# A fused attention and two-MLP kernel: the first six attention tiles put in source order, with small steps moved from GpSimd to VectorE

## The chip, the cores and the metric

The kernel runs as one program on one core of a Trainium2 chip. The metric is the time of one execution in device microseconds; a kernel's time is the median of its runs.

## What is computed

Inputs are float32, the MLP weights float64. Three stages follow one another on 4 sequences of 768 tokens with 8 heads of 48 (a model width of 384).

```python
# 1. linear attention with a decaying state, per batch and head
for t in range(768):
    cur = outer(u * k[t], v[t])
    y[t] = r[t] @ (state + cur)
    state = w[:, None] * state + outer(k[t], v[t])
# 2. a gated MLP with a 3-tap convolution over time
h = maximum(x @ w_in, 0)                       # 384 -> 1024
conv = sum(conv_w[j] * shifted(h, j - 1) for j in range(3))
x = (h * sigmoid(conv)) @ w_out                # 1024 -> 384
# 3. layer norm, MLP, residual
xn = (x - mean) / sqrt(var + 1e-6) * g_ln
out = x + maximum(xn @ w_ch1, 0) @ w_ch2       # 384 -> 1536 -> 384
```

## The kernel before

Attention is done in 24 tiles of 128 tokens, 6 for each batch. The first MLP (`mixer1`) works on 8 blocks of 384 tokens, which are three attention tiles each, and the second (`mixer2`) on 6 blocks of 512. Products that need full precision are split into a high and a low part, and three matmuls are made of each.

*Attention tiles.* A generator, `attention`, yields after each half tile; the main loop calls `step()` to take one. The first six tiles (`n < LIGHT`, LIGHT is 6) go through `light_tile`. For such a tile VectorE (DVE in the profile) scales r and k by a decay table (`rk`, line 347), multiplies them (`z`, line 302) and makes the decayed k (`kks`, line 247, `decayed_k`). TensorE (PE) makes the dot products `dps` and the diagonal `pa8`. ScalarE (ACT) copies them (`aT`, `a8`), GpSimd (POOL) masks `aT` and makes `va`. PE adds them up in `yps`; ACT writes the high part `xh`, PE takes it away with the matrix `minus`, and ACT writes the low part `xl`. `halos` then copies single columns between neighbouring blocks, since the convolution needs one token on each side: when tile 3 is done, its first column goes into the last column of block 0's `xh` and `xl`. `state_update` makes the next state: `pst` on PE, `sn` on DVE, the decayed state `sw` (line 396, on POOL for the first six tiles), and two ACT copies `sbds`.

*Weights.* The float64 weights are decoded on the chip in 22 pieces (`wjob`). A piece is loaded into `st`; ACT takes the magnitude of its upper words (Abs, `wdec<-st`), an engine clamps it (`magnitude`, TENSOR_SCALAR `wdec<-wdec` in float32), DVE shifts it (TENSOR_SCALAR in int32) and combines it twice (SCALAR_TENSOR_TENSOR), ACT writes the high part (`wih`, `woh`), DVE the low part (`wil`, `wol`). The next piece's Abs and clamp are issued between the second combination and the high part. `me` is a piece's number: 0 to 2 are the first half of `w_in`, 3 is the first rows of `w_out`, 4 to 6 the second half of `w_in`, 7 to 9 the rest of `w_out`, 10 to 21 belong to the second MLP. In the kernel before, pieces 0 to 3 are clamped on DVE and the others on POOL. `wdo` takes decode steps; in the start loop two are taken after each `step()`, until piece 3 is done, and two at each call in block 0.

*Order.* Each engine works through its own queue in order. Instructions issued through the wrappers `vo`, `ao`, `so`, `go` and `pe` (of the class `InOrder`) are kept behind the instruction that was issued just before them on their engine. All of PE's instructions and the weight decode are issued so. Those issued through the plain names `v_`, `a_`, `g_` and `nc.sync` may be put earlier by a scheduler at compile time, as soon as its own estimate has their inputs ready, but no later than the next kept one. The attention's DVE, ACT and POOL instructions and the tile loads are of this kind. Loads are issued by SP.

*Start.* `tables` loads the small inputs and tiles 0 to 2, builds the decay tables, and makes `tku[:, 0]` through a PE transpose (`ptk`, from `tkw`) and two ACT copies (line 697); `decayed_k(0)` needs this table. Then comes:

```python
    cst = tables()
    decayed_k(0)
    while finished[0] < EARLY - 1:   # EARLY is 4
        step()
        wdo(2, wo_job[0])
```

Of the kernel before, what the change touches and what calls it, by code (L numbers as in the profile page):

```python
# [32 lines left out]
NP = H // 2  # L33
# [15 lines left out]
def body(ctx, tc, r, k, v, w, u, w_in, conv_w, w_out, g_ln, w_ch1, w_ch2, rkT, krv, small, out):  # L49
# [89 lines left out]
    def wjob(src, n, hi, lo, scale=None):  # L139

        st, mag = [], []

        def load():
            st.append(io.tile([128, 2 * WN], I32, tag="st", name="st", bufs=3))
            dst = st[0][:, 0:2 * n]
            if len(src.shape) == 3:
                dst = dst.rearrange("p (a n) -> p a n", a=src.shape[1])
            so.dma_start(out=dst, in_=src.bitcast(I32))

        def ahead():  # L150
            if not mag:
                mag.append(magnitude(st[0], n, vo if me < 4 else go))

        def steps():
            ahead()
            t = mag[0]
            yield from decode(st[0], n, t)
            if me + 1 < min(len(wjobs), w_loaded[0]):
                wjobs[me + 1][2]()
            if len(src.shape) == 3:  # L160
                t = t.rearrange("p (a n) -> p a n", a=src.shape[1])
            kw = {} if scale is None else {"scale": gl[:, scale:scale + 1]}
            ao.activation(out=hi, in_=t, func=AF.Copy, **kw)
            yield
            if scale is None:
                vo.tensor_tensor(out=lo, in0=t, in1=hi.bitcast(F32), op=ALU.subtract)
            else:
                vo.scalar_tensor_tensor(out=lo, in0=t, scalar=kw["scale"], in1=hi.bitcast(F32),
                                        op0=ALU.mult, op1=ALU.subtract)
        me = len(wjobs)  # L170
        wjobs.append((load, steps(), ahead))
        return len(wjobs) - 1

# [70 lines left out]
    def decayed_k(n):  # L244

        if n < LIGHT:
            v_.tensor_tensor(out=kks[:, n % 2, 0, :, 0:D], in0=loaded[n][1], in1=tku[:, 0], op=ALU.mult)
            return
        v_.tensor_tensor(out=kks[:, n % 2, :, :, 0:D], in0=loaded[n][1].unsqueeze(1).to_broadcast([128, 2, H, D]), in1=tku,  # L249
                         op=ALU.mult)  # L250
# [28 lines left out]

    def halos(n, xh, xl):  # L280
        i, j = n % TPB, n // TT
        for t, e in ((xh, 0), (xl, 1)):
            if i == 0:
                g_.memset(t[:, :, 0:1].bitcast(F32), 0.0)
            if i == TPB - 1:
                g_.memset(t[:, :, T + 1:T + 2].bitcast(F32), 0.0)
            if n % TT == 0 and i > 0:
                g_.tensor_copy(out=xT[j - 1][e][:, :, T + 1:T + 2], in_=t[:, :, 1:2].bitcast(F32))  # L288
                g_.tensor_copy(out=t[:, :, 0:1], in_=xT[j - 1][e][:, :, T:T + 1].bitcast(F32))

    def dot_products(rT, kT):
        dps = [ps_a.tile([128, NP, C], F32, tag="pa", name="dps") for _ in range(2)]
# [5 lines left out]

    def light_tile(n, rk, vt, py, py_tag):
        rT, kT = rk[:, 0], rk[:, 1]  # L300
        z = ap.tile([PR, NP, C], F32, tag="z", name="z", bufs=2)
        v_.tensor_tensor(out=z, in0=rT, in1=kT, op=ALU.mult)
        yield

        dps = dot_products(rT, kT)
        pb, pb_tag = (ps_m, "m") if n < EARLY else (ps_a, "pa")
        pa8 = pb.tile([128, 512], F32, tag=pb_tag, name="pa8")[:, 0:H]
        for p in range(NP):
            pe.matmul(pa8[:, 2 * p:2 * p + 2], lhsT=z[:, p, :], rhs=ub[:, 2 * p:2 * p + 2], start=True, stop=True)
        aT = ap.tile([128, 2, NP, C], F32, tag="aT", name="aT", bufs=2)  # L310
        a8 = sp.tile([128, H, 1], F32, tag="a8", name="a8", bufs=2)
        for q in range(2):
            a_.activation(out=aT[:, q], in_=dps[q], func=AF.Copy)
            g_.affine_select(out=aT[:, q], in_=aT[:, q], compare_op=ALU.is_gt, fill=0.0, base=0,
                             pattern=[[0, NP], [1, C]], channel_multiplier=-1)
        a_.activation(out=a8.rearrange("x h o -> x (h o)"), in_=pa8, func=AF.Copy)
        va = ap.tile([128, H, D], F32, tag="av", name="va", bufs=2)
        g_.tensor_tensor(out=va, in0=vt[:, :, 0:D], in1=a8.to_broadcast([128, H, D]), op=ALU.mult)
        yield

        yps = py.tile([128, KT, C], F32, tag=py_tag, name="yps")
        products(n, yps, rT, vt, aT)
        for kk in range(KT):
            pe.matmul(yps[:, kk, :], lhsT=va.rearrange("x h d -> x (h d)")[:, kk * 128:kk * 128 + 128], rhs=ident,
                      start=False, stop=True, skip_group_check=True)
        j = n // TT
        xh, xl = xT[j] if j in xT else new_xT(j)
        sl = slice(1 + (n % TT) * C, 1 + (n % TT) * C + C)
        a_.activation(out=xh[:, :, sl], in_=yps, func=AF.Copy)
        load_tile(n + 3)  # L330
        if n + 2 < NT:
            decayed_k(n + 2)
        yield

        pe.matmul(yps, lhsT=minus, rhs=xh[:, :, sl], start=False, stop=True, skip_group_check=True)
        a_.activation(out=xl[:, :, sl], in_=yps, func=AF.Copy)
        halos(n, xh, xl)
        finished[0] = n
        yield

    def attn_tile(n):
        b, i = divmod(n, TPB)
        rk, _, rt, vt = loaded[n]
        py, py_tag = (ps_c, "acc") if n < EARLY else (ps_a, "pa")

        rT, kT = rk[:, 0], rk[:, 1]
        v_.tensor_tensor(out=rk, in0=rk, in1=trk, op=ALU.mult)  # L347
        if n < LIGHT:
            yield from light_tile(n, rk, vt, py, py_tag)
            return  # L350
        av = ap.tile([128, H, D], F32, tag="av", name="av", bufs=2)
        v_.tensor_tensor(out=av, in0=kks[:, n % 2, 1, :, 0:D], in1=rt, op=ALU.mult)  # L352
        a8 = sp.tile([128, H, 1], F32, tag="a8", name="a8", bufs=2)
        v_.tensor_reduce(out=a8.rearrange("x (q p) o -> x q (p o)", q=2), in_=av.rearrange("x (p q) d -> x q p d", q=2),  # L354
                         axis=AX.X, op=ALU.add)
        aT = ap.tile([128, 2, NP, C], F32, tag="aT", name="aT", bufs=2)
        g_.affine_select(out=aT.rearrange("x q p c -> x (q p) c"), in_=a8.to_broadcast([128, H, C]),  # L357
                         compare_op=ALU.is_equal, fill=0.0, base=0, pattern=[[0, H], [1, C]], channel_multiplier=-1)
        yield

        dps = dot_products(rT, kT)
        for q in range(2):
            v_.copy_predicated(out=aT[:, q], mask=later.bitcast(I32).unsqueeze(1).to_broadcast([128, NP, C]), data=dps[q])  # L363
        yield

        yps = py.tile([128, KT, C], F32, tag=py_tag, name="yps")
        products(n, yps, rT, vt, aT)
        j = n // TT
        xh, xl = xT[j] if j in xT else new_xT(j)
        sl = slice(1 + (n % TT) * C, 1 + (n % TT) * C + C)  # L370
        a_.activation(out=xh[:, :, sl], in_=yps, func=AF.Copy)
        v_.tensor_tensor(out=xl[:, :, sl], in0=yps, in1=xh[:, :, sl].bitcast(F32), op=ALU.subtract)  # L372
        load_tile(n + 3)
        if n + 2 < NT:
            decayed_k(n + 2)
        halos(n, xh, xl)
        finished[0] = n
        yield

    def state_update(n):  # L380
        first, last = n % TPB == 0, n % TPB == TPB - 1
        vt = loaded[n][3]
        if not last:
            pst = ps_a.tile([128, NP, D], F32, tag="pa", name="pst")
            for h in range(H):
# [7 lines left out]
                v_.tensor_tensor(out=sn, in0=pst[0:PR], in1=state[0], op=ALU.add)  # L393
            if n % TPB < TPB - 2:
                state[0] = ap.tile([PR, NP, D], F32, tag="sw", name="sw")
                (g_ if n < LIGHT else v_).tensor_tensor(out=state[0], in0=sn, in1=w128.to_broadcast([PR, NP, D]),
                                                        op=ALU.mult)
            sb = sbd[(n + 1) % 2]
            a_.activation(out=sb[0:D, :, 0:D], in_=sn[0:D], func=AF.Copy)
            a_.activation(out=sb[64:PR, :, D:2 * D], in_=sn[64:PR], func=AF.Copy)  # L400
# [250 lines left out]
    def tables():  # L651
        nc.sync.dma_start(out=smallt, in_=small)
        load_tile(0)
        nc.sync.dma_start(out=tku[:, 1], in_=u.unsqueeze(0).to_broadcast([128, H, D]))
        wload(1)
        load_tile(1)
        wload(2)
        cst = ap.tile([128, 6 * NF1], I32, tag="cst", name="cst", bufs=1)
        nc.sync.dma_start(out=cst, in_=conv_w.bitcast(I32))
        load_tile(2)  # L660
        wload(3)
        make_identity(nc, ident)
        for t in (kks[:, 0, 0], kks[:, 1, 0]):
            g_.memset(t[:, :, D:64], 0.0)
# [83 lines left out]

    cst = tables()
    decayed_k(0)  # L750
    while finished[0] < EARLY - 1:
        step()
        wdo(2, wo_job[0])
# [124 lines left out]
```

## Time and profile before

| what | value |
|---|---|
| median of 3 runs (lowest to highest) | 669.76 us (665.53 to 671.35) |
| the profiled execution's own time | 668.53 us |
| its span in the profile | 666.8 us |
| PE busy | 629.3 us (94%) |
| DVE busy | 431.7 us (65%) |
| ACT busy | 264.3 us (40%) |
| POOL busy | 135.1 us (20%) |

Times in the rows are microseconds from the start of the span. The execution's own time is 1.7 us longer than its span. PEclk is the clock granted to TensorE, as a share of full speed. PE is one queue; PEld is its weight loads. A row of the timeline has the start, the duration, the engine, the line, the operation with what it writes and reads, how many instructions were merged, and in brackets how long the engine had been idle and what ended that.

### The profile page before, as it was taken

The page shows a single profiled execution, that of the slowest core. Times are in us where ns is not written, and L with a number is a line of the kernel's source. Part 1 is how long each engine was busy: PE and PEld are TensorE (multiplying, and loading weights), DVE is VectorE, ACT ScalarE, POOL GpSimd, SP SyncE. Part 2 cuts the span into 40 slices and gives each one's busy share as a digit, 9 for nine tenths or more (in the row PEclk, how much of TensorE's full clock was granted, in tenths as well). Part 3 has the DMA queues.
Part 4 walks back from the last instruction along what each step waited for, and adds up shares of the span by engine and source line. Part 5 has one row for each costly group of instructions (what it writes and reads, how often), then busy time and mean ns, then how long its engine had stood idle before and what let it go on. Part 6 is the DMA issues. An engine that isn't in the chain of part 4 may idle for free.

```text
span 666.8 us, 11692 instructions
## 1 busy us (share of the span) xinstructions
PE 629.3 (94%) x4782; PEld 574.1 (86%) x4782; DVE 431.7 (65%) x772; ACT 264.3 (40%) x518; POOL 135.1 (20%) x142
## 2 busy tenths in 40 slices
PE   5879689999989899999999999999999999999996
PEld 4769579889879898899998999999999999999996
DVE  7887999999999998988788852422422422421211
ACT  3356656455654565566665521221211121121110
POOL 5374642230321213011007510100100100100000
PEclk9978799999989899999999999999999999999999
DMA  8663616235254434102043301101100200200101
GB/s 275 201 211 109 218 41 211 87 101 173 74 161 132 138 102 132 43 2 83 14 167 115 110 1 48 47 1 56 40 1 23 72 1 13 83 1 1 47 1 52
DMA packets 25294, 56.50 MB, mean 85 GB/s; under 512 B 2961, under 2 KB 15378, under 8 KB 25234
## 3 DMA queue, kind: packets, MB, share of 16 engines
q1 hardware_dynamic: 25234, 55.68, 26.3%
q8 instruction: 39, 0.64, 0.4%
q14 instruction: 21, 0.17, 0.1%
HBM read 46.24 MB, written 9.44 MB: 83 GB/s over the span
## 4 chain that ended last, share of the span: by engine, by line
PE 62%; DVE 24%; DMA 6%; issue 3%; ACT 3%; POOL 1%; SPq 1%; DVEq 0%; ACTq 0%
PE psm L75 30%; PE acc L75 30%; DVE c L474 6%; DMA rk<-in_rkT_dram 5%; DVE wdec L75 4%; DVE c L455 2%; DVE aT L363 2%; DVE rk L347 2%; DVE gl L461 2%; PE yps L75 1%; PE pxt L75 1%; DVE av L352 1%; DVE kks L249 1%; DVE a L354 1%; DVE xl L372 1%
## 5 line engine op out<-in xcount | busy, mean ns | idle before, releaser
L488 DVE SCALAR_TENSOR_TENSOR rl<-psm,rh 128x512 fp32r<-128x512 f32 x72 | 49.6, 689 | 133.0 <-ACT rh L487 129.5
L487 ACT ACTIVATE rh<-psm 128x512 fp32r<-128x512 f32 x72 | 43.1, 599 | 193.7 <-PE psm L75 190.1
L75 PE MATMUL acc<-c2h,rh 128*128 128x384 f32 x288 | 97.1, 337 | 0.0
L75 PE MATMUL acc<-c2l,rh 128*128 128x384 f32 x288 | 97.0, 337 | 0.0
L75 PE MATMUL acc<-c2h,rl 128*128 128x384 f32 x288 | 97.0, 337 | 0.0
L474 DVE SCALAR_TENSOR_TENSOR c<-h,tables,c 128x384 f32<-128x384 f32 x128 | 87.0, 685 | 7.4 <-ACT c L472 6.8
L75 PE MATMUL psm<-xnh,c1h 128*128 128x512 f32 x216 | 86.6, 401 | 0.0
L75 PE MATMUL psm<-xnh,c1l 128*128 128x512 f32 x216 | 84.9, 393 | 0.0
L75 PE MATMUL psm<-xnl,c1h 128*128 128x512 f32 x216 | 84.6, 392 | 0.0
L75 PE MATMUL psm<-xh,wih 128*128 128x386 f32 x192 | 70.0, 364 | 7.5 <-DVE aT L363 3.2
L75 PE MATMUL acc<-woh,gh 128*128 128x384 f32 x192 | 68.1, 355 | 2.7 <-ACT x L496 2.7
L75 PE MATMUL acc<-wol,gh 128*128 128x384 f32 x192 | 65.8, 343 | 4.2 <-DVE wol L75 4.2
L75 PE MATMUL psm<-xl,wih 128*128 128x386 f32 x192 | 67.4, 351 | 2.4 <-POOL xl L288 2.4
L75 PE MATMUL acc<-woh,gl 128*128 128x384 f32 x192 | 66.1, 344 | 1.8 <-DVE gl L461 1.8
L75 PE MATMUL psm<-xh,wil 128*128 128x386 f32 x192 | 67.3, 351 | 0.5 <-DVE wil L75 0.5
L75 POOL TENSOR_SCALAR wdec<-wdec 128x768 f32<-128x768 f32 (+2 forms) x19 | 55.3, 2911 | 50.8 <-ACT wdec L75 41.3
L511 POOL TENSOR_TENSOR rs<-rs,nhalf 128x1 f32<-128x1 f32 x24 | 15.5, 654 | 230.5 <-DVE rs L510 229.9
L75 PEld LDWEIGHTS acc<-c2l,rh 128*128 128x128 f32 x288 | 54.1, 188 | 3.0
L75 PEld LDWEIGHTS acc<-c2h,rh 128*128 128x128 f32 x288 | 54.1, 188 | 2.8
L75 PEld LDWEIGHTS acc<-c2h,rl 128*128 128x128 f32 x288 | 54.0, 188 | 0.0
L454 ACT ACTIVATE c<-c 128x384 f32<-128x384 f32 x64 | 33.4, 521 | 44.0 <-DVE c L474 43.5
L357 POOL TENSOR_SCALAR_AFFINE_SELECT aT<-a 128x1024 f32<-128x1024 f32 x18 | 29.1, 1617 | 104.0 <-PE yps L75 45.1
(115 smaller groups left out, 1144.2 us busy)
## 6 DMA issues: line engine op xcount, KB each, us to landing
rk<-in_rkT_dram SPq DMA_DIRECT2D x24, 448.0 KB, 5.0
st<-in_moe_w_ch_dram SPq DMA_DIRECT2D x12, 768.0 KB, 5.9
rv<-in_krv_dram SPq DMA_DIRECT2D x18, 448.0 KB, 4.8
kt<-in_krv_dram SPq DMA_DIRECT2D x24, 192.0 KB, 2.8
x_dram<-x SPq DMA_DIRECT2D x24, 192.0 KB, 2.0
x1b<-x_dram SPq DMA_DIRECT2D x24, 192.0 KB, 3.5
out_dram<-x1b SPq DMA_DIRECT2D x24, 192.0 KB, 2.3
st<-in_moe_w_in_dram SPq DMA_DIRECT2D x6, 512.0 KB, 6.1
```

The source lines that it names most:

```text
L75: return lambda *args, **kw: tc.keep_in_program_order(op(*args, **kw))
L249: v_.tensor_tensor(out=kks[:, n % 2, :, :, 0:D], in0=loaded[n][1].unsqueeze(1).to_broadcast([128, 2, H, D]), in1=tku, op=ALU.mult)
L347: v_.tensor_tensor(out=rk, in0=rk, in1=trk, op=ALU.mult)
L357: g_.affine_select(out=aT.rearrange("x q p c -> x (q p) c"), in_=a8.to_broadcast([128, H, C]), compare_op=ALU.is_equal, fill=0.0, base=0, ...
L363: v_.copy_predicated(out=aT[:, q], mask=later.bitcast(I32).unsqueeze(1).to_broadcast([128, NP, C]), data=dps[q])
L454: a_.activation(out=st["c"], in_=st["c"], func=AF.Sigmoid)
L455: v_.tensor_tensor(out=st["c"], in0=st["h"][:, 1:T + 1], in1=st["c"], op=ALU.mult)
L461: v_.tensor_tensor(out=st["gl"], in0=st["c"], in1=st["gh"].bitcast(F32), op=ALU.subtract)
L474: v_.scalar_tensor_tensor(out=c, in0=h[:, o:o + T], scalar=cw[:, tap, f:f + 1], in1=c, op0=ALU.mult, op1=ALU.add)
L487: a_.activation(out=gh[:, 0:cols], in_=ps[:, 0:cols], func=AF.Relu)
L488: v_.scalar_tensor_tensor(out=gl_[:, 0:cols], in0=ps[:, 0:cols], scalar=0.0, in1=gh[:, 0:cols].bitcast(F32), op0=ALU.max, op1=ALU.subtract)
L511: g_.tensor_tensor(out=rs[:, 1:2], in0=rs[:, 0:1], in1=nhalf, op=ALU.pow)
```

## The change

Five edits: the early tiles' attention instructions on DVE, ACT and POOL are issued through the kept-in-order wrappers; the halos of tiles 0 to 4 and the state decay of the first six tiles go from POOL to DVE; the clamps of weight pieces 4 to 9 go from POOL to DVE; in `tables` the loads of tiles 1 and 2 are issued ahead of the table of u, the convolution weights and all but the first weight piece; and one `step()` is taken ahead of the start loop, so that in source order the weight decode begins one half tile later.

```diff
@@ def wjob
         def ahead():
             if not mag:
-                mag.append(magnitude(st[0], n, vo if me < 4 else go))
+                mag.append(magnitude(st[0], n, vo if me < 10 else go))
@@ def decayed_k(n)
         if n < LIGHT:
-            v_.tensor_tensor(out=kks[:, n % 2, 0, :, 0:D], in0=loaded[n][1], in1=tku[:, 0], op=ALU.mult)
+            ordered(n)[0].tensor_tensor(out=kks[:, n % 2, 0, :, 0:D], in0=loaded[n][1], in1=tku[:, 0], op=ALU.mult)
             return
@@ def halos(n, xh, xl)
         i, j = n % TPB, n // TT
+        g_ = vo if n <= EARLY else nc.gpsimd
@@
+    def ordered(n):
+        return (vo, ao, go) if n < LIGHT else (nc.vector, nc.scalar, nc.gpsimd)
+
@@ def light_tile
         rT, kT = rk[:, 0], rk[:, 1]
+        v_, a_, g_ = ordered(n)
@@ def attn_tile(n)
-        v_.tensor_tensor(out=rk, in0=rk, in1=trk, op=ALU.mult)
+        ordered(n)[0].tensor_tensor(out=rk, in0=rk, in1=trk, op=ALU.mult)
@@ def state_update(n)
         vt = loaded[n][3]
+        v_, a_, g_ = ordered(n)
@@
-                (g_ if n < LIGHT else v_).tensor_tensor(out=state[0], in0=sn, in1=w128.to_broadcast([PR, NP, D]),
-                                                        op=ALU.mult)
+                v_.tensor_tensor(out=state[0], in0=sn, in1=w128.to_broadcast([PR, NP, D]), op=ALU.mult)
@@ def tables
         load_tile(0)
+        load_tile(1)
+        wload(1)
+        load_tile(2)
+        wload(3)
         nc.sync.dma_start(out=tku[:, 1], in_=u.unsqueeze(0).to_broadcast([128, H, D]))
-        wload(1)
-        load_tile(1)
-        wload(2)
         cst = ap.tile([128, 6 * NF1], I32, tag="cst", name="cst", bufs=1)
         nc.sync.dma_start(out=cst, in_=conv_w.bitcast(I32))
-        load_tile(2)
-        wload(3)
@@ the start
     decayed_k(0)
+    for _ in range(1):
+        step()
     while finished[0] < EARLY - 1:
         step()
         wdo(2, wo_job[0])
```

## Rows read from the trace of the kernel before

**Rows 1.** The page's head and its first part.

```profile
span 666.8 us, 11692 instructions
...
PE 629.3 (94%) x4782; PEld 574.1 (86%) x4782; DVE 431.7 (65%) x772; ACT 264.3 (40%) x518; POOL 135.1 (20%) x142
```

**Rows 2.** Stretches: length, busy of PE, PEld, DVE, ACT, POOL, then PEclk, DMA.

```profile
9.00:20.90 11.90, 11.90 (x102) 10.64 (x102) 7.89 (x9) 4.26 (x10) 5.63 (x9) 1.00 0.91 294
...
31.20:38.00 6.80, 6.80 (x84) 5.84 (x83) 4.54 (x7) 4.07 (x9) 3.83 (x5) 0.50 0.65 222
...
44.80:55.00 10.20, 6.66 (x23) 5.78 (x26) 7.72 (x11) 4.78 (x11) 6.56 (x11) 0.50 0.28 102
...
72.10:78.90 6.80, 5.71 (x17) 5.20 (x18) 6.80 (x12) 4.47 (x8) 5.81 (x2) 0.50 0.87 256
...
260.00:661.00 401.00, 400.36 (x2338) 368.76 (x2330) 192.08 (x374) 123.96 (x231) 45.14 (x38) 1.00 0.14 45
```

**Rows 3.** The same view, most of the first mixer1 block.

```profile
70.00:100.00 30.00, 22.61 (x173) 20.03 (x177) 29.66 (x48) 17.85 (x34) 16.04 (x8) 0.89 0.41 121
```

**Rows 4.** Timeline of PE from 7 to 84 us.

```profile
8.86 2.08 PE L75 MATMUL dps<-rk 48*128 48x128 f32 x16 [0.46 <-DVE rk L347]
...
19.36 1.65 PE L75 MATMUL yps<-tables,va 128*128 128x128 f32 x6
...
29.21 0.44 PE L75 MATMUL yps<-xh,minus 128*128 128x384 f32 x1 [1.97 <-ACT xh L329]
...
45.98 0.69 PE L75 MATMUL psm<-xh,wih 128*128 128x386 f32 x1 [1.14 <-POOL xh L288]
49.07 0.69 PE L75 MATMUL psm<-xl,wih 128*128 128x386 f32 x1 [2.41 <-POOL xl L288]
...
72.73 0.69 PE L75 MATMUL psm<-xh,wih 128*128 128x386 f32 x1 [2.96 <-ACT wih L75]
...
83.60 0.44 PE L75 MATMUL acc<-wol,gh 128*128 128x384 f32 x1 [2.52 <-DVE wol L75]
```

**Rows 5.** Timeline of ACT from 8 to 30 us.

```profile
8.44 0.55 ACT L697 ACTIVATE tables<-ptk 128x192 f32<-128x192 f32 x2 [6.03 <-PE ptk L75]
...
17.80 0.68 ACT L75 ACTIVATE wdec<-st 128x512 f32<-128x512 f32 x1
21.04 0.49 ACT L329 ACTIVATE xh<-yps 128x384 fp32r<-128x384 f32 x1 [2.56 <-PE yps L75]
```

**Rows 6.** Timeline of DVE from 7 to 100 us.

```profile
7.57 2.36 DVE L347 TENSOR_TENSOR rk<-rk,tables 112x1024 f32<-112x1024 f32 x2 [0.30 <-POOL tables L685]
...
17.88 1.23 DVE L247 TENSOR_TENSOR kks<-kt,tables 128x384 f32<-128x384 f32 x1 [1.93 <-DMA kt<-in_krv_dram]
...
21.82 0.88 DVE L75 TENSOR_SCALAR wdec<-wdec 128x512 f32<-128x512 f32 x2
...
36.60 0.98 DVE L75 TENSOR_SCALAR wdec<-wdec 128x768 f32<-128x768 f32 x1 [2.23 <-ACT wdec L75]
...
45.17 3.80 DVE L347 TENSOR_TENSOR rk<-rk,tables 112x1024 f32<-112x1024 f32 x1
...
49.16 0.94 DVE L249 TENSOR_TENSOR kks<-kt,tables 128x768 f32<-128x768 f32 x1
...
53.27 1.64 DVE L474 SCALAR_TENSOR_TENSOR c<-h,tables,c 128x384 f32<-128x384 f32 x2 [2.16 <-ACT c L472]
...
68.26 1.04 DVE L75 TENSOR_SCALAR wdec<-wdec 128x512 int32<-128x512 int32 x1
```

**Rows 7.** Groups by shape, POOL, 7 to 130 us: busy, mean ns, idle before.

```profile
L75 POOL TENSOR_SCALAR wdec<-wdec 128x768 f32<-128x768 f32 x4 | 12.0, 2988 | 6.8 <-ACT wdec L75 6.7
...
L396 POOL TENSOR_TENSOR sw<-sn,w 112x192 f32<-112x192 f32 x4 | 6.7, 1676 | 11.9 <-DVE sn L393 11.6 <-ACT sn L391 0.3
L75 POOL TENSOR_SCALAR wdec<-wdec 128x512 f32<-128x512 f32 x3 | 6.7, 2223 | 4.4 <-DVE c L474 3.6 <-ACT wdec L75 0.8
```

**Rows 8.** Groups by shape, DVE, 7 to 55 us.

```profile
L302 DVE TENSOR_TENSOR z<-rk 112x512 f32<-112x512 f32 x6 | 4.3, 709 | 0.2
...
L393 DVE TENSOR_TENSOR sn<-pst,sw 112x192 f32<-112x192 f32 x4 | 1.4, 350 | 0.0
```

## The prediction

> **What bounds the kernel now.** I read the head of the page first, then the stretches, then the timeline of each engine where PE waits. From 260 us on PE is busy 400.36 of 401.00 us [rows 2]; nothing of the change reaches that part except by when it begins. The change can act on the part before, in two places. Up to the first block of mixer1, PE works through the attention tiles and then stands before the first matmuls: the one at 45.98 waited 1.14 us and the one at 49.07 2.41 us, both for halo copies in POOL's queue, and earlier one at 29.21 waited 1.97 us for an ACT copy [rows 4]. From 70 to 100 us PE is busy 22.61 of 30.00 us while DVE is busy 29.66 [rows 3]: here DVE is the bound, and PE's waits at 72.73 (2.96 us) and 83.60 (2.52 us) are for decoded weights [rows 4]. So what counts is how early DVE gets through its work, and the page's 65% for DVE [rows 1] hides that.
>
> PE's clock adds to it: at 0.50 (1.2 GHz instead of 2.4) in 31.2 to 38.0, 44.8 to 55.0 and 72.1 to 78.9 us [rows 2], each time around one of these waits.
>
> **The profile's time.** The profiled execution took 668.53 us, 1.7 us more than its span of 666.8 [rows 1]; the median is 669.76, 1.2 us above. The sum below gives a difference, which I put on the median.
>
> **Part 1, source order at the front: a loss of 2.0 us on PE.** `decayed_k(0)` is called before the first step. It needs the table that ACT finishes at 8.44 + 0.55 = 8.99 us [rows 5]. Before, rk of tile 0 ran ahead of it at 7.57 and the dot products began at 8.86 [rows 4, 6]. Kept in order, rk of tile 0 is queued behind that kks: 8.99 + about 0.55 (half of the 0.94 that twice the columns took, plus a little) + 1.2 for rk (2.36 for two) [rows 6] puts the dot products at 10.8. All of PE is queued behind them.
>
> **Part 2, where the weight decode starts: a loss of 2.4 us.** From 8.86 to the end of the first yps at 19.36 + 1.65 = 21.0 PE had no gap, 12.15 us [rows 4], busy 11.90 of 11.90 from 9 us on [rows 2]; 2.0 us later that is 23.0. Before, the Abs of weight piece 0 ran at 17.80, ahead of the first xh at 21.04 [rows 5], and its clamp on DVE at 21.82 [rows 6]. With one step taken first, that Abs is traced after xh and kept behind it: 23.0 + 0.49 + 0.68 [rows 5] = 24.2, the clamp at 24.3. If PE's clock rises earlier in its work than it did, up to 1 us of this returns.
>
> The loads cost nothing here. kks of tile 2 waited 1.93 us for its k, until 17.88 [rows 6]; the same bytes lie ahead of that load, so it lands as late. In source order tile 2's kks, rk and z now stand ahead of the clamp, done by 17.9 + 0.6 + 1.2 + 0.7 = 20.4 [rows 6, 8], with 3.9 us of cover from the wait for xh. Without the cover each us that k comes later costs one. Piece 0 now queues behind tile 1's V instead of the table of u, some tenths of a us on a load that is not used before 23.5. On SP, the table of u and the convolution weights go behind the weight loads; the table of u is first used by the kks of tile 6, just ahead of the rk at 45.17 [rows 6].
>
> **Part 3, DVE from the first clamp to the last halo.** I count by difference. Before, DVE went from the clamp at 21.82 to 45.17 [rows 6], 23.35 us, of which it waited 2.23 (at 36.60, a clamp behind its Abs): 21.1 of work. Off: rk and z of tile 5 (1.2 + 0.7) and the kks of tile 6 (0.95), which had been put ahead and now come later, 2.85 in all. On: rk and z of tile 3, 1.9; the clamp of piece 4, 0.44 (two instructions in 0.88 at 21.82); three state decays at the 0.35 of sn, which has their shape [rows 8], 1.05; the last sn, 0.35; six halo instructions, which the trace shows on POOL alone, between nothing and 0.2 each: 0.6. That is 22.6 us. Waits in order: the clamp of piece 1 stands behind its Abs, and on ACT ahead of that Abs now stand two state copies that wait for sn, xl, two aT copies and a8. From the walk of these queues DVE waits 1.8 us there; the nearest row is the 2.23 at 36.60. At the end the last xl stands behind aT, a8 and the state copies on ACT, and the halo waits about 1.2. Sum: 24.3 + 22.6 + 1.8 + 1.2 = 49.9. Before, the matmul that needs this halo ran at 49.07 [rows 4]: plus 0.8.
>
> So the 3.55 us of waiting for POOL's halos do go, and what is late next is DVE itself, by the same amount and a little more.
>
> **Part 4, what DVE still owes then.** Before, it had rk and z of tile 5, the kks of tiles 6 and 7 and the rk of tile 6 done by 50.1 (3.80 us for that rk, beside POOL's halos and masks) and waited 2.16 us at 53.27 for the first block [rows 6]. After, 1.9 us for tile 5 and some 3.0 for the others are left, against about 3.2 us of free time before the block's first DVE work: 1.7 us of backlog.
>
> **Part 5, the clamps of pieces 5 to 9 in block 0.** On POOL they took 2.2 us for 512 columns and 3.0 for 768 [rows 7], none of it on DVE's queue. On DVE: two at 0.44 and three at about 0.66 (half as many columns again; the 0.98 at 36.60 is the upper end) are 2.9 us. Against that stands what a POOL clamp does to DVE: beside one, the shift at 68.26 took 1.04 instead of 0.44, and the two combinations at 53.27 took 1.64 where the group's mean is 0.685 each, 0.3 to 0.6 us for each clamp [rows 6]. Five return 1.5 to 3.0; I take 2.4, since the larger clamps run longer. Net plus 0.5, with ends of minus 0.1 and plus 3.5 (nothing returned, all at 0.98).
>
> The skill has two rules here, and they point opposite ways. The Trainium skill, "SBUF — State Buffer", section "Who interferes with whom", says that a DVE instruction with two SBUF inputs and a GpSimd instruction that reads SBUF block each other; the 3.80 us rk agrees, and by it the sum would be the one with everything returned. The Trainium skill, "Perfetto Trace Analysis", section "Optimizing Scalar/DVE Operations", advises taking work off a saturated DVE, to GpSimd even, with the warning that the shared port may eat the gain; by it the change goes the wrong way, and the sum would be the upper end.
>
> **Sum.** 0.8 + 1.7 + 0.5 = plus 3.0 us at the end of block 0, where DVE is the bound; PE, which waits for it there, ends that much later, and from 260 us on nothing gives it back. 669.76 + 3.0 is 672.8; I say 672.5.
>
> **Rivals.**
> *The queues run free (faster).* If the two in-order waits of part 3 (3.0 us) and part 1's delay do not add, because an ACT copy or PE's clock is earlier than I count, the first block starts 3 to 4 us earlier than 49.07. PE then has no long wait from 40 to 50 us and may keep 2.4 GHz: of 44.8 to 55.0 it was busy 6.66 us at half speed [rows 2], which is worth 3. With the decode ahead, part of the 2.96 us at 72.73 goes too. Together about 8: 662. For it: POOL's halos, decays and clamps are the long items of its queue. Against it: DVE has no slack to run ahead with.
> *Clamps wait for Abs (slower).* On DVE a clamp holds up everything behind it, combination and gating alike, until ACT has run the Abs. At 36.60 this cost 2.23 us [rows 6]; pieces 5 to 9 add five such places in a stretch where DVE has no time to lose. At four of five times that price, 9 us: 681. It decides from the point where ACT reaches an Abs later than DVE finishes the combination before it. For it: 36.60. Against it: ACT is busy 17.85 of 30 us there [rows 3], so mostly it is early.
> *Nothing is returned (slower, small).* POOL's masks and va still run beside DVE, so DVE pays for the clamps in full: plus 3.5 instead of 0.5, and 676.
>
> **How the numbers follow.** About 1%, 6.7 us, is what a measurement of this kernel can tell from no change. The forecast has 0.45, with a range of its own of 667 to 677 from the ends of parts 2 and 5 and the one wait not counted; the free queues 0.28, the waiting clamps 0.15, nothing returned 0.12. Nearly all of the first rival is faster by over 1%; the second is slower, with half of the last. Faster 0.27, same 0.51, slower 0.22. The range runs from 661 to 680, which leaves out a tenth at each side.
>
> **What would show it.** Part 1: the first dot products at 10.8 instead of 8.86. Part 2: the first clamp at 24 or later, right behind xh and Abs on ACT. Part 3: no wait of PE for POOL before the first psm, the halos on DVE, and the second psm at 49 to 51; if it comes before 46, the first rival holds. Part 4: rk of tile 5 behind the halos. Part 5: idle time of DVE ahead of clamps from 50 to 100 us, released by ACT, is the second rival; combinations and shifts back at 0.7 and 0.4 us are the return. The prediction is wrong if DVE falls idle before 46 us with its list done, or if PE's waits at 72.73 and 83.60 change by more than 3 us.

## The result and the profile after

The changed kernel takes 673.37 us (median of 16 runs, 671.76 to 678.5) against 667.66 us for the kernel before (16 runs, 665.44 to 671.35): ratio 1.009, 95% interval 1.0075 to 1.0106. That is 5.7 us slower, where the sum of the prediction gave 3.0. The profiled execution of after took 675.25 us, 1.9 above its median; that of before was 0.9 above its own [rows 1]. So about 1 us of the 6.7 between the two spans (673.5 and 666.8 us) belongs to the single executions.

The head of the page after, answering to [rows 1]: POOL gave up 15 us of work, DVE took 4.0 more.

```profile
span 673.5 us, 11674 instructions
...
PE 632.3 (94%) x4782; PEld 578.2 (86%) x4782; DVE 435.7 (65%) x788; ACT 263.8 (39%) x518; POOL 120.0 (18%) x126
```

The stretches of after (columns as in [rows 2]):

```profile
9.00:20.90 11.90, 10.18 (x96) 9.43 (x96) 7.12 (x9) 3.58 (x9) 4.70 (x6) 1.00 1.01 309
20.90:31.10 10.20, 10.20 (x111) 8.66 (x103) 5.74 (x14) 4.73 (x10) 2.85 (x6) 1.00 0.07 16
31.10:44.80 13.70, 13.08 (x236) 11.06 (x228) 13.27 (x22) 6.80 (x15) 3.42 (x4) 1.00 0.96 293
44.80:58.40 13.60, 7.24 (x23) 6.03 (x27) 11.81 (x23) 6.49 (x15) 5.81 (x5) 0.50 0.48 158
...
70.00:100.00 30.00, 23.88 (x216) 21.23 (x214) 29.37 (x45) 16.90 (x33) 6.02 (x7) 0.89 0.46 143
...
260.00:667.00 407.00, 405.34 (x2365) 373.68 (x2365) 198.52 (x385) 127.02 (x237) 47.04 (x40) 1.00 0.13 44
```

Read the DVE column (the third) first. From 20.9 to 31.1 us it is busy 5.74 of 10.20; from 31.1 to 44.8 us it is nearly full. What it misses early it can make up only in part: before had 2.3 us of free time between 31.2 and 38.0 us and 2.5 between 44.8 and 55.0 [rows 2], and none to speak of from 70 to 100 us [rows 3]. From 260 us on PE is as full as before [rows 2]: the loss is all made ahead of that.

The timeline of PE in after, answering to [rows 4]:

```profile
10.72 2.08 PE L75 MATMUL dps<-rk 48*128 48x128 f32 x16 [2.37 <-DVE rk L75]
...
24.45 2.08 PE L75 MATMUL dps<-rk 48*128 48x128 f32 x16
...
33.19 1.16 PE L75 MATMUL dps<-rk 48*128 48x128 f32 x16
...
41.56 1.16 PE L75 MATMUL dps<-rk 48*128 48x128 f32 x16
...
47.48 0.69 PE L75 MATMUL yps<-xh,minus 128*128 128x384 f32 x1 [3.17 <-ACT xh L75]
50.51 0.66 PE L75 MATMUL psm<-xh,wih 128*128 128x386 f32 x1 [2.34 <-DVE xh L75]
52.51 0.69 PE L75 MATMUL psm<-xl,wih 128*128 128x386 f32 x1 [1.34 <-DVE xl L75]
...
64.51 0.44 PE L75 MATMUL psm<-xh,wih 128*128 128x386 f32 x1 [1.51 <-ACT aT L75]
...
77.40 1.16 PE L75 MATMUL dps<-rk 48*128 48x128 f32 x14 [3.20 <-ACT xl L75]
...
88.12 0.44 PE L75 MATMUL acc<-wol,gh 128*128 128x384 f32 x1 [1.93 <-DVE wol L75]
...
100.83 0.44 PE L75 MATMUL acc<-woh,gl 128*128 128x384 f32 x1 [1.71 <-DVE gl L466]
```

PE's order is the same in both kernels, so the k-th instruction of a name can be set against the k-th. In after the first dot products are late by 1.86 us (10.72 against 8.86 [rows 4]), the fifth tile's by only 0.78 (41.56 against 40.78 in before), the second psm by 3.44 (52.51 against 49.07), the matmul that waits for the low half of the out weights by 4.52 (88.12 against 83.60), the first of mixer2 by 6.08 (355.07 against 348.99). So PE made good most of its late start by 41 us. What stays is lost behind that: 3.44 us by 52 us, and most of the rest in the first block, where the matmul at 100.83 is 6.36 us late (94.47 in before).

The timeline of DVE in after, answering to [rows 6]:

```profile
8.98 0.56 DVE L75 TENSOR_TENSOR kks<-kt,tables 128x384 f32<-128x384 f32 x1 [1.75 <-ACT tables L701]
...
16.04 0.36 DVE L75 TENSOR_TENSOR sw<-sn,w 112x192 f32<-112x192 f32 x1 [2.31 <-ACT sn L75]
18.80 0.59 DVE L75 TENSOR_TENSOR kks<-kt,tables 128x384 f32<-128x384 f32 x1 [2.40 <-DMA kt<-in_krv_dram]
...
24.13 0.89 DVE L75 TENSOR_SCALAR wdec<-wdec 128x512 f32<-128x512 f32 x2 [1.94 <-ACT wdec L75]
...
29.34 0.88 DVE L75 TENSOR_SCALAR wdec<-wdec 128x512 f32<-128x512 f32 x1 [2.31 <-ACT wdec L75]
...
46.89 1.22 DVE L352 TENSOR_TENSOR rk<-rk,tables 112x1024 f32<-112x1024 f32 x1
48.03 0.95 DVE L75 TENSOR_TENSOR wol<-wdec,woh 128x768 fp32r<-128x768 f32 x1
48.90 0.95 DVE L249 TENSOR_TENSOR kks<-kt,tables 128x768 f32<-128x768 f32 x1
49.77 0.35 DVE L75 TENSOR_TENSOR sn<-pst,sw 112x192 f32<-112x192 f32 x1
50.03 0.40 DVE L75 CAST xh<-xh 128x3 fp32r<-128x3 f32 x2
50.35 1.39 DVE L249 TENSOR_TENSOR kks<-kt,tables 128x768 f32<-128x768 f32 x1
51.67 0.86 DVE L75 CAST xl<-xl 128x3 fp32r<-128x3 f32 x2
52.44 1.21 DVE L75 TENSOR_TENSOR rk<-rk,tables 112x1024 f32<-112x1024 f32 x1
...
56.66 1.27 DVE L479 SCALAR_TENSOR_TENSOR c<-h,tables,c 128x384 f32<-128x384 f32 x2 [1.55 <-ACT c L477]
...
61.39 0.56 DVE L460 TENSOR_TENSOR c<-h,c 128x384 f32<-128x384 f32 x1 [1.22 <-ACT c L459]
```

The first five rows are the five long waits of DVE, 10.7 us in all, each with another instruction at the head of the queue: ACT's table, ACT's state copy, k's load, the Abs of piece 0, the Abs of piece 1. From the clamp of piece 1 to the last halo its longest gap is 0.22 us. At the end of the list stand the low half of piece 3, wol at 48.03 (in before it ran at 43.44), and the halos between rk and kks of tiles 6 and 7, which are not among the first six and so not kept in order.

ACT in after, answering to [rows 5]; then the table load ahead of the first gating (the sigmoid of mixer1); and last the copy that ends PE's wait at 77.40, behind a weight piece that waits for DVE:

```profile
22.91 0.49 ACT L75 ACTIVATE xh<-yps 128x384 fp32r<-128x384 f32 x1 [3.21 <-PE yps L75]
23.43 0.66 ACT L75 ACTIVATE wdec<-st 128x512 f32<-128x512 f32 x1
...
59.54 1.28 ACT L459 ACT_TABLE_LOAD   x1
...
76.33 0.63 ACT L75 ACTIVATE wih<-wdec 128x512 fp32r<-128x512 f32 x1 [0.97 <-DVE wdec L75]
76.87 0.48 ACT L75 ACTIVATE xl<-yps 128x384 fp32r<-128x384 f32 x1
```

### The profile page after: what moved, and what is told of

The parts are those of the page before. It is cut to its first block, busy times and chain, and to the rows that moved or that the text cites. A ratio compares the mean times of both kernels' runs of the same rounds, so it can differ in the third digit from the quotient of the medians.

```text
span 673.5 us, 11674 instructions
## 1 busy us (share of the span) xinstructions
PE 632.3 (94%) x4782; PEld 578.2 (86%) x4782; DVE 435.7 (65%) x788; ACT 263.8 (39%) x518; POOL 120.0 (18%) x126
## 4 chain that ended last, share of the span: by engine, by line
PE 70%; DVE 20%; DMA 4%; ACT 3%; issue 2%; SPq 0%; DVEq 0%; ACTq 0%
PE acc L75 31%; PE psm L75 31%; DVE c L479 5%; DMA rk<-in_rkT_dram 4%; DVE wdec L75 3%; PE yps L75 3%; PE dps L75 2%; DVE c L460 2%; DVE aT L368 1%; DVE rk L352 1%; PE pxt L75 1%; DVE gl L466 1%; DVE kks L249 1%; PE pst L75 1%; PE pa L75 1%
## 5 line engine op out<-in xcount | busy, mean ns | idle before, releaser
L479 DVE SCALAR_TENSOR_TENSOR c<-h,tables,c 128x384 f32<-128x384 f32 x128 | 89.8, 705 | 7.2 <-ACT c L477 6.5
L75 PE MATMUL psm<-xh,wih 128*128 128x386 f32 x192 | 70.5, 367 | 6.7 <-DVE aT L368 2.8
L362 POOL TENSOR_SCALAR_AFFINE_SELECT aT<-a 128x1024 f32<-128x1024 f32 x18 | 27.2, 1511 | 123.8 <-PE yps L75 69.5
L465 ACT ACTIVATE gh<-c 128x384 fp32r<-128x384 f32 x64 | 33.4, 523 | 40.4 <-DVE c L460 39.9
L75 POOL TENSOR_SCALAR wdec<-wdec 128x768 f32<-128x768 f32 (+1 forms) x13 | 41.7, 3210 | 41.2 <-ACT wdec L75 37.3
```

Source lines behind the costliest of these rows:

```text
L75: return lambda *args, **kw: tc.keep_in_program_order(op(*args, **kw))
L465: a_.activation(out=st["gh"], in_=st["c"], func=AF.Copy)
L479: v_.scalar_tensor_tensor(out=c, in0=h[:, o:o + T], scalar=cw[:, tap, f:f + 1], in1=c, op0=ALU.mult, op1=ALU.add)
```

## The experiments

Two theories stood at first. A: the source order itself costs the time, through waits at the head of the queues in front. B: the work moved to VectorE (halos, state decay, clamps) costs it. Later C: ScalarE's order, by tiles 4 and 5, makes the waits of PE in the first mixer1 block; and V against S: VectorE's order or ScalarE's. The table has before, after and all twelve experiments. "DVE idle" is the sum of the gaps ahead of its instructions from 7 us to the end of wol of piece 3, added up from its timeline; "end" is that end; "psm" the start of the second psm matmul.

| kernel | VectorE in source order | DVE idle, us | end, us | psm, us | ratio to before (95%) |
|---|---|---|---|---|---|
| before | no | 6.9 | 44.4 | 49.07 | 1 |
| after | yes | 11.4 | 49.0 | 52.51 | 1.0090 (1.0075 to 1.0106) |
| order_only | yes | 14.2 | 47.5 | 54.32 | 1.0111 (1.0082 to 1.0140) |
| order_vector | yes | 13.7 | 46.7 | 53.40 | 1.0090 (1.0060 to 1.0120) |
| no_first_step | yes | 12.7 | 46.9 | 52.08 | 1.0093 (1.0061 to 1.0126) |
| kks0_later | yes | 11.6 | 48.9 | 52.42 | 1.0120 (1.0096 to 1.0145) |
| clamps_pool | yes | 11.7 | 49.1 | 52.67 | 1.0088 (1.0054 to 1.0122) |
| tiles45_free | tiles 0 to 3 | 11.3 | 51.2 | 53.88 | 1.0199 (1.0164 to 1.0234) |
| order_scalar | no | 7.5 | 45.5 | 51.99 | 1.0039 (1.0020 to 1.0058) |
| moves_only | no | 7.8 | 45.7 | 50.33 | 1.0061 (1.0039 to 1.0084) |
| small_moves_only | no | 7.8 | 45.4 | 50.09 | 1.0004 (0.9978 to 1.0029) |
| clamps_only | no | 8.9 | 45.2 | 49.75 | 1.0006 (0.9985 to 1.0028) |
| loads_first | no | 7.4 | 44.6 | 49.31 | 0.9989 (0.9967 to 1.0011) |
| early_decode | no | 8.1 | 45.0 | 54.91 | 1.0025 (1.0004 to 1.0046) |

Every kernel with VectorE in source order has 11.3 us of idle or more and a ratio of 1.0088 or more; every kernel without has 8.9 or less, and 1.0061 or less. Inside the two groups no column ranks the kernels: tiles45_free has the least idle time of its group and by far the highest ratio, and early_decode has the latest psm of all at 1.0025. DVE is busy for the same time up to there in after and in before (49.0 - 7 - 11.4 = 30.6 and 44.4 - 7 - 6.9 = 30.5 us): the 4.6 us by which the list ends later are idle time. The same holds up to the wol that PE waits for in block 0, at 88.07 in after and 83.55 in before: 15.6 us idle against 10.8. But order_scalar (15.1) and early_decode (15.2) have lost as much by there, at 1.0039 and 1.0025. So idle time tells where the delay up to a point comes from, not how much of it the whole time keeps.

### The order alone and the moves alone

The kernel before with the order of the first six tiles on all three engines, and nothing else of the change (order_only):

```diff
+    def ordered(n):
+        return (vo, ao, go) if n < LIGHT else (nc.vector, nc.scalar, nc.gpsimd)
... (its calls as in the change)
```

> The kernel before with the early tiles' attention instructions kept in source order, and nothing else of the change: no first step, loads as before, halos, state decay and clamps on GpSimd as before. Theory A: the order costs without the moves too; with the first step left out the ratio is 1.003 to 1.010. Theory B: order by itself costs nothing: 0.997 to 1.001.

The kernel before with halos, state decay and clamps on VectorE, no order (moves_only):

```diff
-                mag.append(magnitude(st[0], n, vo if me < 4 else go))
+                mag.append(magnitude(st[0], n, vo if me < 10 else go))
...
+        g_ = vo if n <= EARLY else nc.gpsimd
...
-                (g_ if n < LIGHT else v_).tensor_tensor(out=state[0], ...)
+                v_.tensor_tensor(out=state[0], ...)
```

> The kernel before with the halos of tiles 0 to 4, the state decay of the first six tiles and the clamps of pieces 4 to 9 on VectorE, and nothing else of the change. Theory A: the waits of 1.14 and 2.41 us for GpSimd's halos go and nothing takes their place, the decode of the later pieces is no later: ratio 0.990 to 0.997. Theory B: VectorE is given some 5 us of work in the stretch where it is the bound and gets less than that back: 1.004 to 1.010.

Measured 1.0111 and 1.0061. The order alone costs at least what the whole change costs, just above A's range, and B's "order by itself costs nothing" is refuted. But the moves are not free together either, and lie in B's range, and the two do not add up to 1.009. The next runs split both.

The order on VectorE alone (order_vector), and on ScalarE alone (order_scalar), with the calls of `ordered` as in the change:

```diff
+        return (vo, nc.scalar, nc.gpsimd) if n < LIGHT else (nc.vector, nc.scalar, nc.gpsimd)
```
```diff
+        return (nc.vector, ao, nc.gpsimd) if n < LIGHT else (nc.vector, nc.scalar, nc.gpsimd)
```

> The kernel before with the early tiles' attention instructions kept in source order on VectorE alone; those on ScalarE and GpSimd float as before. All the order together gave 1.011, with VectorE idle for 14.2 us from 7 us to the low part of piece 3 instead of 6.9. Theory V (VectorE's own order makes the idle time: the first kks ahead of rk, a clamp ahead of the rk that could run): ratio 1.007 to 1.012, the first dot products at 10.7, and idle time of 10 us or more. Theory S (ScalarE's order makes it: Abs and high parts queued behind and ahead of the attention's copies): 0.999 to 1.004.

> The same with the order on ScalarE alone. Theory V: 0.998 to 1.004, the first dot products at 8.9. Theory S: 1.006 to 1.012, with VectorE waiting for Abs 2 us or more in two or three places, and PE for xl near 77 us.

Measured 1.009 and 1.0039. DVE's timeline with its order alone shows the form of the loss:

```profile
9.15 0.56 DVE L75 TENSOR_TENSOR kks<-kt,tables 128x384 f32<-128x384 f32 x1 [1.75 <-ACT tables L702]
...
20.62 0.99 DVE L75 TENSOR_SCALAR wdec<-wdec 128x512 f32<-128x512 f32 x2 [6.65 <-ACT wdec L75]
...
22.73 1.22 DVE L75 TENSOR_TENSOR rk<-rk,tables 112x1024 f32<-112x1024 f32 x1
```

One clamp waits 6.65 us for its Abs, and rk of tile 2, whose data had landed at 14.5 us, stands behind it and behind the kks of its tile, whose k landed at 19.5; in before this rk ran at 13.21. Without the order the longest wait up to there was 1.93 us [rows 6]. ScalarE's order alone gives less than half the loss, with a wait for POOL's halos at the front and one of 4.88 us, for ACT's xl, in block 0 at 75.61. PE of order_scalar:

```profile
51.99 0.69 PE L75 MATMUL psm<-xl,wih 128*128 128x386 f32 x1 [4.17 <-POOL xl L288]
```

V holds as the main part: this one edit gives the whole loss. That S adds to it in the full change isn't shown: after, with both, is no slower than order_vector, and the intervals of order_only and order_vector overlap.

How VectorE's order costs time is less certain than that it does. The seven kernels with it share something else: in block 0 ACT runs the second slice's h and c ahead of the first slice's gating and its table load, and DVE waits 0.63 to 1.22 us for the gating (1.22 at 61.39 in after). In the seven others the table load stands ahead of the second h, and DVE waits 0.07 us at most. ACT of before:

```profile
53.83 1.28 ACT L454 ACT_TABLE_LOAD   x1
```

The second h follows at 55.55; in after it runs at 58.38, the load at 59.54. These instructions of mixer1 are not kept in order in any kernel, so it is the compile-time scheduler that placed them. No run separates this from the waits at the front.

### Parts 1 and 2 undone one at a time

After without the extra step ahead of the loop (no_first_step); after with the first kks behind the rk and z of tile 0 (kks0_later):

```diff
     decayed_k(0)
-    for _ in range(1):
-        step()
```
```diff
         go_on(0)
+        decayed_k(0)
         decayed_k(1)
...
-    decayed_k(0)
```

> The changed kernel without the extra step ahead of the start loop. Theory A (the loss comes from the source order at the front: the first kks ahead of rk, the first Abs behind xh, tile 6 and 7 work ahead of the last halo): the first Abs runs at about 19.8 us, right behind the a8 of tile 1 at 19.53, instead of 23.43, the first clamp at about 20.5 instead of 24.13, and the second matmul of the first block some 2 to 3 us before 52.51; ratio to the kernel before 1.005, between 1.002 and 1.008. Theory B (the loss comes from the work that was moved from GpSimd to VectorE, which is the bound before 100 us): the decode starts earlier but VectorE has the same work, so the ratio stays at 1.008 to 1.010.

> The changed kernel with the kks of tile 0 issued behind the rk and z of tile 0 instead of ahead of them. Theory A: the first dot products start at 8.9 us instead of 10.72, the first Abs at about 21.5 instead of 23.43, and up to 1.9 us of the loss of 5.7 us goes: ratio 1.006, between 1.004 and 1.008. Theory B: VectorE is the bound from the first clamp on, and a start that is 1.9 us earlier is worth at most 1 us: 1.008 to 1.010.

Both gave back the start that they were to give back, and no time: 1.0093 and 1.012. The first lies in B's range, the second above both, so A's two causes at the front fail when they are taken one at a time. In no_first_step the first clamp ran at 20.46, 3.7 us earlier, after a wait of 4.04; piece 3 was done at 46.9 instead of 49.0; the second psm gained 0.43. In kks0_later the dot products began at 8.71 and the first clamp ran at 21.90, and DVE's waits moved on:

```profile
18.54 0.56 DVE L75 TENSOR_TENSOR kks<-kt,tables 128x384 f32<-128x384 f32 x1 [4.17 <-DMA kt<-in_krv_dram]
...
46.00 1.23 DVE L352 TENSOR_TENSOR rk<-rk,tables 112x1024 f32<-112x1024 f32 x1 [1.86 <-DMA rk<-in_rkT_dram]
```

(Both rows are DVE's.) DVE reached k's load earlier and waited 4.17 us there instead of 2.40: its idle time is 11.6 us, as in after (11.4). Later PE stood 7.30 us at 81.41 for ACT's xl. An early start is worth nothing to an in-order queue whose next item isn't there.

### Tiles 4 and 5 out of the order

```diff
-        return (vo, ao, go) if n < LIGHT else (nc.vector, nc.scalar, nc.gpsimd)
+        return (vo, ao, go) if n < EARLY else (nc.vector, nc.scalar, nc.gpsimd)
```

> The changed kernel with tiles 4 and 5, which run beside the first block of mixer1, taken out of the order; tiles 0 to 3 stay in it. Theory C (in the first block the order hurts on ACT: xl of tile 4 at 76.87 stands behind a high part that waits for VectorE, and PE stands 3.20 us for it at 77.40, and 1.51 us at 64.51 behind aT of tile 5): both waits go, xl of tile 4 runs within 5 us of its PSUM being ready, ratio 1.002 to 1.006. Theory A, the front alone: those waits come out as another wait for weights, ratio 1.008 to 1.010.

Measured 1.0199, the slowest of all and outside both ranges. The wait of 3.20 us at 77.40 is gone, and PE waits for weights instead. PE of tiles45_free:

```profile
77.94 0.45 PE L75 MATMUL psm<-xh,wih 128*128 128x386 f32 x1 [1.08 <-ACT wih L75]
...
80.30 0.44 PE L75 MATMUL psm<-xh,wil 128*128 128x386 f32 x1 [1.74 <-DVE wil L75]
...
88.60 0.44 PE L75 MATMUL acc<-wol,gh 128*128 128x384 f32 x1 [2.15 <-DVE wol L75]
```

With rk and z of tile 4 free to run ahead, DVE ended piece 3 at 51.2 instead of 49.0: the decode came later by what was put ahead of it. C falls as the sole cause. Why it is so slow is only half seen: at 88.60 PE is 5.0 us late (83.60 in before), at the first of mixer2 10.4 (359.35), and no run takes the second half apart.

### The moves one at a time

Clamps of pieces 4 to 9 on VectorE in the kernel before (clamps_only), and back on POOL in after (clamps_pool):

```diff
-                mag.append(magnitude(st[0], n, vo if me < 4 else go))
+                mag.append(magnitude(st[0], n, vo if me < 10 else go))
```
```diff
-                mag.append(magnitude(st[0], n, vo if me < 10 else go))
+                mag.append(magnitude(st[0], n, vo if me < 4 else go))
```

> The kernel before with the clamps of pieces 4 to 9 on VectorE and nothing else. If the clamps make the loss of 1.006 that all moves together showed, this is at 1.004 to 1.008, with the wait for wol near 84 us at 3 us or more; if they return what they cost, 0.998 to 1.002, and the halos and the decay make the loss.

> The changed kernel with the clamps of pieces 4 to 9 back on GpSimd. Theory B (VectorE pays for the clamps): the ratio falls from 1.009 to 1.003 to 1.006. Theory A or C (the clamps return on VectorE what they cost): 1.008 to 1.012; the price of 0.5 us that was predicted for them lies below what can be told.

Measured 1.0006, and 1.0088 against after's 1.009: no worth of the clamps can be told from nothing, either way. The sign for a loss, a wait for wol of 3 us or more near 84 us, did come (3.27 at 83.92), without the loss. Groups by shape, DVE, 55 to 105 us of clamps_only (busy, mean ns, idle before):

```profile
L75 DVE TENSOR_SCALAR wdec<-wdec 128x768 f32<-128x768 f32 x3 | 1.7, 559 | 0.0
...
L75 DVE TENSOR_SCALAR wdec<-wdec 128x512 f32<-128x512 f32 x2 | 0.8, 418 | 0.0
```

Five clamps cost DVE 2.5 us and not one stands idle before it; POOL had spent 2.2 to 3.0 us on each [rows 7]. That the time stays speaks for about as much coming back to DVE from the instructions that had run beside POOL's clamps. The trace shows some of it: from 53 to 103 us the four av took 0.55 us each instead of 0.88, and the three shifts of 512 columns 0.42 instead of 0.62; but other groups grew (the three wil from 0.68 to 0.98), so no balance can be struck from the rows.

Halos and state decay on VectorE, nothing else (small_moves_only):

```diff
+        g_ = vo if n <= EARLY else nc.gpsimd
...
-                (g_ if n < LIGHT else v_).tensor_tensor(out=state[0], ...)
+                v_.tensor_tensor(out=state[0], ...)
```

> The kernel before with the halos of tiles 0 to 4 and the state decay of the first six tiles on VectorE and nothing else. If the halos there stand behind the rk and kks of tiles 6 and 7, which are put ahead of them, the first block begins as late as with GpSimd: the second matmul at 49 to 51 us, and the ratio is 0.999 to 1.005. If the way is free, it begins at 46 to 47 and the ratio is 0.992 to 0.996.

Measured 1.0004. PE's waits for POOL's halos of 1.14 and 2.41 us [rows 4] became 2.93 (at 48.51) and 0.92 us (at 50.09) for DVE's, since DVE has rk and kks of tiles 6 and 7 ahead of the halos. DVE of small_moves_only:

```profile
46.19 1.65 DVE L348 TENSOR_TENSOR rk<-rk,tables 112x1024 f32<-112x1024 f32 x1
...
48.03 0.39 DVE L75 CAST xh<-xh 128x3 fp32r<-128x3 f32 x2
48.34 1.61 DVE L249 TENSOR_TENSOR kks<-kt,tables 128x768 f32<-128x768 f32 x1
49.87 0.25 DVE L75 CAST xl<-xl 128x3 fp32r<-128x3 f32 x2
```

Each move alone shows no cost, all together 1.0061. Why they don't add up is open: in moves_only the matmul that waits for wol in block 0 runs at 86.11, after a wait of 3.35 us, 2.5 us later than in before; in clamps_only it runs at 83.92 and in small_moves_only at 84.05, 0.3 and 0.4 late. No run takes this apart.

### The loads alone, and the decode earlier

The load order of the change in the kernel before (loads_first), and, as a try at the opposite of part 2, a first piece of decode inside the attention's start in the kernel before (early_decode):

```diff
         load_tile(0)
+        load_tile(1)
+        wload(1)
+        load_tile(2)
+        wload(3)
         nc.sync.dma_start(out=tku[:, 1], in_=u.unsqueeze(0).to_broadcast([128, H, D]))
...
```
```diff
         go_on(0)
+        wdo(2, wo_job[0])
         go_on(1)
```

> The kernel before with the loads of tiles 1 and 2 ahead of the table of u, the convolution weights and all but the first weight piece, and nothing else. The prediction costs this at nothing: ratio 0.998 to 1.002, the first clamp at 21 to 23 us. If the loads matter, rk and V of tile 2 land earlier and the ratio is 0.995 or less, or the weight pieces land later and it is 1.004 or more.

> The kernel before with the first two decode steps (Abs, clamp, shift and first combination of piece 0) taken inside the first step, behind the a8 of tile 0, so that they come earlier in source order; nothing else is changed. If when VectorE gets its first weight work sets the start (theory A in its present form: idle time of VectorE up to the first block is what counts), the first clamp runs at 16 to 17 us instead of 21.8, the low part of piece 3 at 41 to 43 instead of 44.4, and the ratio is 0.993 to 0.998. If the waits only move to the next clamp, 0.999 to 1.003.

Measured 0.9989: no cost of the loads. And 1.0025: the first clamp ran at 16.58, 5.2 us earlier than in before, and the time did not fall; wol of piece 3 ended at 45.0, not at 41 to 43, and theory A in that form fails. The step that starts the decode also stood ahead of a load on SP's queue: the load of tile 4's rk was issued at 29.26 us instead of 24.95, and DVE waited for it. DVE of early_decode:

```profile
16.58 1.06 DVE L75 TENSOR_SCALAR wdec<-wdec 128x512 f32<-128x512 f32 x2
...
34.18 1.23 DVE L347 TENSOR_TENSOR rk<-rk,tables 112x1024 f32<-112x1024 f32 x1 [4.54 <-DMA rk<-in_rkT_dram]
```

At block 0's wol matmul (88.58) PE was 4.98 us late here, more than in after (4.52); at the first of mixer2 it was 3.24 late (352.23 against 348.99), in an execution 1.6 us above its median. A delay at that point can shrink again before mixer2.

No kernel here beats the one before.

## Why the prediction was right, and where it was too small

**Part 1** came as written: first dot products at 10.72 us (10.8 predicted). **Part 2** too: on ACT the Abs stands right behind xh, at 23.43, and the clamp runs at 24.13 (24.3). What PE lost by them it mostly had back by 41.56 us (0.78 late), as before had lost time there on its own: the wait of 1.97 us at 29.21 [rows 4] and the half clock from 31.2 to 38.0 [rows 2], neither of which after has. PE's clock did not help, as part 2 allowed that it might (last section). The runs that undo the two parts singly give no time back.

**Part 3** held in kind. PE waits for no halo of POOL, DVE is what is late, the clamp of piece 1 waits 2.31 us (1.8 counted), and the second psm starts at 52.51 (49.9 predicted, 49 to 51 allowed). These 2.6 us are **part 4**, paid early: rk of tile 6 and both kks (1.22 + 0.95 + 1.39 = 3.56 us of DVE) ran ahead of the last halo and not behind it. The waits were counted about right: from 24.13 to the end of the last halo at 52.53 DVE was idle 2.9 us (1.8 + 1.2 = 3.0 counted) and busy 25.5 (22.6 counted). Parts 3 and 4 together gave 0.8 + 1.7 = 2.5 us at the first block; measured are 3.4, by the second psm and by the first c (56.66 against 53.27 [rows 6]). The other 0.9 us comes of the place: ahead of the halo the work delays the block in full, while the free time that part 4 set against it, ahead of the first c, was left over (1.55 us idle at 56.66).

**Part 5** held, as far as can be told: net plus 0.5 was forecast for the clamps, clamps_only shows 1.0006, +0.4 us with an interval of -1.0 to +1.9. The Trainium skill, "Perfetto Trace Analysis", section "Optimizing Scalar/DVE Operations", warns that moving work between GpSimd and DVE might not help as they share a port; the ratio agrees, in this direction as well.

**The sum** is the step that was too small. It let the block add nothing to what arrives there but the clamps' 0.5 us, because DVE had no time to lose in it. Measured are 5.7 - 3.4 = 2.3 us by the medians (6.08 - 3.44 = 2.6 by the profiles). Some 1.1 of them can be read off as idle time. At 88.12 as at 83.60 PE waits for DVE's wol, so DVE is the bound up to there, and it is 4.52 us late instead of the 3.39 at the first c. Between the two, DVE stood idle 1.07 us longer: 2.48 us from 56.66 to 88.12 by its stretches, against 1.41 from 53.27 to 83.60 in before. The new waits are 0.56 us at 59.56 and 1.22 at 61.39, both for ACT's work on the first two slices; the longer one goes with the order on ACT that the experiments showed. PE's half clock there is not new: 44.8 to 58.4 us in after, 44.8 to 55.0 in before [rows 2].

Behind 88 us one more step can be seen. The next wol of the block is no later than the last (98.68 against 94.20, 4.48 us), but then PE waits 1.71 us at 100.83 for DVE's gl, which in before cost no wait, and is 6.36 us late. In before that gl ran at 90.90, ahead of the wol at 93.20; in after at 100.24, behind the wol at 97.68. The same wait stands in no_first_step (1.83 us), kks0_later (1.56) and tiles45_free (0.50); order_vector and clamps_pool have none, so it appears where the order and the clamps are both on VectorE. From there the delay moves between 5.8 and 8.9 us and is 6.08 at mixer2, which no run takes apart. PE's wait of 1.51 us for ACT's aT at 64.51, and the half clock right behind it (0.51 from 65.3 to 68.7 us by the stretches, where ten matmuls took 2.80 us and in before 1.89 at a granted 1.00), make PE 5.75 us late at 67.31; by 88.12 it is 4.52, so they are hidden behind the wait for the weights.

That the forecast of 672.5 us lies so near to the measured 673.37 is in part luck: it was added to a time of before of 669.76 from 3 runs, and 16 runs gave 667.66. Of the difference, 5.7 us, the sum has about half.

**The rivals.** The free queues did not come: DVE's list ended 4.6 us later. Clamps waiting for Abs were not seen in the block; DVE's waits there are for ACT's work on the slices, and one of 0.63 us at 85.98 for a load. Nothing returned would have cost clamps_only some 2.5 us, the clamps' own time on DVE; its interval ends at 1.9. That the waits at 72.73 and 83.60 would change by no more than 3 us held, the first barely: it went from 2.96 us to nothing (the matmul ran at 80.25 without a wait, behind the one of 3.20 us for ACT's xl at 77.40), the second from 2.52 to 1.93 at 88.12.

## What to carry to other kernels

Where one engine's list sets the end, count its idle time up to the last item that others need, and not only when the list starts: here three kernels moved the start by 2 to 5 us and none gained. Writing out the order of such a queue makes each late input a wait for all that stands behind it, and relieving one wait hands its time to the next. An engine that reaches a stretch late is not sure to be busy in it: what feeds it there starts late as well, and a compile-time scheduler may have put the rest in another order.

## What the hardware showed beside it

PE's dot products took 2.08 us for 16 at 24.45 in after and 1.16 at 21.96 in before, though PE had been busy without a gap since 10.72 (10.18 and 10.20 us in the two stretches) and began only 1.86 us later. The granted clock reads 1.00 in both, the level of 2.4 GHz, so that here the instruction's duration shows what the row of the clock does not: the trace's first entry of the clock stands at 31.12 us in after and at 20.92 in before, and ahead of it the 1.00 rests on none. At 33.19 they took 1.16.

One of POOL's masks, beside back-to-back work on DVE, was drawn out more than DVE's rk beside POOL (3.80 us in before [rows 6], 1.22 in after). Two pairs of 128x512, in after:

```profile
27.92 1.23 POOL L75 TENSOR_SCALAR_AFFINE_SELECT aT<-aT 128x512 f32<-128x512 f32 x2 [6.20 <-ACT aT L75]
...
64.53 5.93 POOL L75 TENSOR_SCALAR_AFFINE_SELECT aT<-aT 128x512 f32<-128x512 f32 x2 [10.73 <-ACT aT L75]
```

At 27.92 DVE stood idle until 29.34, and each mask took 0.64 us. From 62 to 70.5 us DVE had no gap; the first mask of the second pair took 4.87 us, but the second, at 69.36, only 1.11. What makes the difference isn't shown.
